# Chunk outputs formed transposed on TensorE, in place of transposes after them, in a delta-rule attention and FFN kernel

## The chip, the cores and the metric

One Trainium2 chip, one core. The metric is the device time of one execution in microseconds (us). Engines are named as in the profile: PE is TensorE, PEld its weight loads, DVE VectorE, ACT ScalarE, POOL GpSimd, SP the engine whose queue issues all DMAs here.

## The reference

Attention with a delta-rule state, then a feed-forward layer, in float32. Sizes: batch B = 4, heads H = 8, sequence S = 768, head size D = 48; 3072 tokens, model width 384, hidden width 2048.

```python
for t in range(S):
    kt, vt, bt = (k_n[:, :, t], v[:, :, t], beta[:, :, t, None])
    y[:, :, t] = np.einsum('bhd,bhde->bhe', q[:, :, t], state)
    v_old = np.einsum('bhde,bhd->bhe', state, kt)
    state = state + bt[:, :, :, None] * np.einsum('bhd,bhe->bhde', kt, vt - v_old)
...
h = x @ w_in
sp = np.maximum(h, 0.0) + np.log1p(np.exp(-np.abs(h)))
g = h * erf(sp)
return (g @ w_out).astype(np.float32)
```

`x` is `y` with the heads of a token side by side (384 features).

## The kernel before

**Tiling.** The sequence is cut into 12 chunks `c` of C = 64 steps. Within a chunk the recurrence is solved as a triangular system, so that a chunk of one batch entry, `j = 4c + b`, 48 in all, needs three sets of small fp32 products: `chain_u` (line 490), `chain_s` (503, the new state) and `chain_y` (517, the output). The 8 heads of a `j` are 4 pairs `p` times 2 halves `hb`; the two halves stand on partitions 0 to 63 and 64 to 127. Four `j` (one chunk of all four batch entries, 256 tokens) make one FFN group `g`, 12 in all.

**FFN.** Each f32 operand is scaled by a power of two and split in two f16 parts. `ffn1` (16 steps of each group) is 9 f16 matmuls of 128x256 (line 707: high by high, high by low, low by high, for 3 k-tiles); `ffn2` (16 steps) is 6 of 128x384 (lines 768 to 770). Between them, for a unit of two steps: `e_sp` (softplus, ACT), `h_out` (copy out of PSUM, DVE or ACT), `e_erf` (ACT), `e_mul` (DVE), `e_split` (f16 high part), `e_rest` (f16 low part, mostly POOL). Softplus and erf lie in different ACT tables; `table()` (line 129) loads one where the last step used the other, so the number of loads follows from the order of steps.

**From chunk output to FFN input, which the change touches.** `chain_y` has `qp` as its 64-column stationary operand and the state and values `zz` as moving operand, so tokens come out on partitions: 8 fp32 matmuls of 128x48 (16 in the trace, as an fp32 matmul is two there), into two column halves of 64. `chain_y2` (522, ACT) copies the 128x192 result out, `chain_m` (528, DVE) takes its largest magnitude per partition. For a group, `x_max`, `x_all` (552, a product that spreads the maxima) and `x_scale` give the scale `sx`. FFN needs features on partitions: `x_tr` (673, 674) transposes with 8 fp32 PE transposes per group, into 2 PSUM banks from the pool `psa` of 3; `x_hi` (690, ACT) and `x_lo` (695, DVE) form the f16 parts from PSUM, each in 6 pieces per group (2 of 128x256, 4 of 64x128).

**Order.** Every step is put in a list (`on(time, function, arguments)`), 2511 steps; the tuple `ORDER` then gives the order in which they are issued. Each engine and the SP queue works through its own instructions strictly in that order; semaphores alone hold it back. 150 `fill` steps are idle matmuls in the first 90 us. Time of a step in `on(...)` has no effect once `ORDER` is there.

Of the kernel before, what the change touches and what calls it, by code (L numbers as in the profile page):

```python
# [7 lines left out]
F32 = mybir.dt.float32  # L8
# [48 lines left out]
YR = 6  # L57
# [12 lines left out]
HSC = 2.0 ** -23  # L70


@with_exitstack
def delta_ffn_kernel(ctx, tc, kT, qT, ktok, vtok, btok, w_in, w_out, cst, out):
    nc = tc.nc
    te, ve, se, ge, sp = nc.tensor, nc.vector, nc.scalar, nc.gpsimd, nc.sync

    con = ctx.enter_context(tc.tile_pool(name="con", bufs=1))
    io = ctx.enter_context(tc.tile_pool(name="io", bufs=2))
    at = ctx.enter_context(tc.tile_pool(name="at", bufs=1))  # L80
    sm = ctx.enter_context(tc.tile_pool(name="sm", bufs=3))
    ff = ctx.enter_context(tc.tile_pool(name="ff", bufs=2))
# [23 lines left out]
    zz = [con.tile([P, NP, 2, D], F32, name=f"z{i}") for i in range(6)]  # L106

    wb = {nm: con.tile([P, NFF + 1, DM], F32, name=f"w_{nm}") for nm in ("in", "out")}
    wv = {nm: w.rearrange("p a b -> p (a b)").bitcast(F16).rearrange("p (a k b) -> p a k b", k=2, b=DM) for nm, w in wb.items()}
    (win_h, win_l), (wout_h, wout_l) = ((v[:, :, 0, :], v[:, :, 1, :]) for v in wv.values())  # L110

    def early(off, n):

        return wb["out"].rearrange("p a b -> p (a b)")[:, off:off + n]

    def r(hb):
        return slice(hb * C, hb * C + C)

# [329 lines left out]
    def merge_m(c, i):  # L448
# [15 lines left out]
    ygrp, mg = {}, {}  # L464
    vt = {}

    def load_v(j):
        c, b = divmod(j, B)
        vt[j] = io.tile([P, NP, D], F32, tag="v", bufs=2, name=f"v{j}")
        sp.dma_start(vt[j], vtok[c][:, b * NP:b * NP + NP, :])  # L470

    def put_v(j):
        c, b = divmod(j, B)
        cs = slice(b * NP, b * NP + NP)
        for hb in range(2):
            h1 = r(1 - hb)
            ge.tensor_tensor(zz[j % 6][h1, :, hb, :], vt[j][h1], st[c]["nm"][h1, cs].unsqueeze(2).broadcast_to([C, NP, D]), op=ALU.mult)  # L477
# [3 lines left out]
    def chain_u(j):  # L481
        c, b = divmod(j, B)
        Z = zz[j % 6]
        pc = pr[j % PB] if j < 2 * B else pbank(f"pc{j}")
        pu = pc[:, :192].rearrange("p (a e) -> p a e", a=NP)
        psn = pc[:, 192:384].rearrange("p (a e) -> p a e", a=NP)
        pcs[j] = pc, pu, psn
        for p in range(NP):
            for hb in range(2):
                te.matmul(pu[r(1 - hb), p, :], xm[c % 2][hb][:, b * NP + p, :], Z[:, p, hb, :], start=True, stop=True)  # L490

    def chain_u2(j):
# [176 lines left out]
    def x_tr(g, i):  # L669
        y = ygrp[g]  # L670
        pv = fg[g]["pt", i] = pbank(f"pt{g}_{i}").rearrange("p (a x) -> p a x", a=2)
        for a in range(2):
            te.transpose(pv[:, a, :P], y[2 * i + a][:, :P], ident)
            te.transpose(pv[:C, a, P:], y[2 * i + a][:, P:], ident)

    def x_parts(g, i):
        G = fg[g]
        pv = G["pt", i]
        js = slice(2 * i, 2 * i + 2)
        return (((slice(0, P), js, slice(0, P)), pv[:, :, :P]),  # L680
                ((slice(0, C), js, slice(P, 192)), pv[:C, :, P:P + C]),
                ((slice(C, P), js, slice(P, 192)), pv[:C, :, P + C:]))

    def x_hi(g, i):
# [7 lines left out]
    def x_lo(g, i):
        G = fg[g]
        for dst, src in x_parts(g, i):
            ve.scalar_tensor_tensor(G["xl"][dst], src, G["sx"][:src.shape[0]], G["xh"][dst], op0=ALU.mult, op1=ALU.subtract)  # L695

    def ffn1(n):
        g, i = divmod(n, NFF)
        G = fg[g]
        if ("ph", i // 2) not in G:  # L700
            G["ph", i // 2] = ps1.tile([P, 2, GT], F32, tag="ph", name=f"ph{g}_{i // 2}")
        ph = G["ph", i // 2][:, i % 2, :]
        m = 0
        for kt in range(3):
            ksl = slice(kt * C, kt * C + C)
            for w, x in ((win_h, "xh"), (win_h, "xl"), (win_l, "xh")):
                te.matmul(ph, w[:, i, kt * P:kt * P + P], G[x][:, :, ksl], start=(m == 0), stop=(m == 8))  # L707
                m += 1
# [190 lines left out]
    for j in range(B * NC_):  # L899
        t = chain_at(j)  # L900
        d = 1.0 if j >= 2 * B else 2.6 / SW / CS
        on(t - 3.3 if j >= 2 * B else t - 1.5, load_v, j)
        on(t - 1.2 if j >= 2 * B else t - 0.7, put_v, j)
        on(t, chain_u, j)
        on(t + 0.2 * d, chain_u2, j)
        if j < B * NC_ - B:
            on(t + CS * d, chain_s, j)
            on(t + (CS + 0.25) * d, chain_s2, j)
        on(t + (CS + 0.05) * d, chain_y, j)
        on(t + (CS + 0.3) * d, chain_y2, j)  # L910
        on(t + (CS + 0.7) * d, chain_m, j)
# [117 lines left out]
```

## Time and profile before

| | us |
|---|---|
| median of 3 runs (669.54 to 673.52) | 670.56 |
| the profiled execution | 671.37 |
| its span, first to last instruction | 669.6 |
| PE busy, of the span | 605.9 |
| DVE busy | 487.1 |
| ACT busy | 447.7 |
| POOL busy | 364.1 |

The first `ffn1` is at 103.7 us, the first `ffn2` at 138.2, the last matmul at 664. A busy PE is counted to the modelled end of each matmul, some 0.2 us after its start, so that short stops between matmuls lie inside the busy time; the spacing of starts shows them.

### The profile page before, as it was taken

What the parts mean: (1) busy time and instruction counts of PE and PEld (TensorE: products, weight loads), DVE (VectorE), ACT (ScalarE), POOL (GpSimd) and SP (SyncE); (2) the same over time, 40 slices, a digit from 0 to 9 for tenths busy, and PEclk for the clock granted to TensorE, in tenths of its full rate; (3) what the DMA queues carried; (4) which work ended last, traced back from release to release, by engine and by line L of the source; (5) the groups of instructions that cost most, each with busy time, mean ns of one, the idle gap of its engine ahead of it and who ended that gap; (6) DMA issues with size and microseconds to landing.
All of it is one profiled execution on the core that took longest, in us unless ns stands there. A gap on an engine that the chain in (4) does not pass through costs nothing.

```text
span 669.6 us, 22927 instructions
## 1 busy us (share of the span) xinstructions
PE 605.9 (90%) x9866; PEld 457.9 (68%) x9866; DVE 487.1 (73%) x1032; ACT 447.7 (67%) x678; POOL 364.1 (54%) x524
## 2 busy tenths in 40 slices
PE   6947898888988989989999999899999999999996
PEld 4634665667775667767777777677677787777674
DVE  4987689897887877888987587676577876554442
ACT  2345697877766735749647878777738858578673
POOL 4172049858689646994359872678663420140222
PEclk9877899999998999989999999999999999999999
DMA  9982592349220287131793122623404410000111
GB/s 240 328 228 78 140 235 52 80 100 173 66 56 2 54 182 153 48 82 34 179 147 75 44 45 49 136 43 85 102 2 94 96 37 14 13 14 1 24 37 24
DMA packets 78981, 60.13 MB, mean 90 GB/s; under 512 B 57504, under 2 KB 66848, under 8 KB 78880
## 3 DMA queue, kind: packets, MB, share of 16 engines
q1 hardware_dynamic: 78880, 58.68, 37.2%
q8 instruction: 77, 1.26, 0.8%
q14 instruction: 24, 0.20, 0.1%
HBM read 46.07 MB, written 12.58 MB: 88 GB/s over the span
## 4 chain that ended last, share of the span: by engine, by line
PE 48%; DVE 25%; ACT 11%; issue 7%; POOL 4%; DMA 3%; SPq 1%; DVEq 0%; ACTq 0%; POOLq 0%
PE ph L707 16%; PE pr L768 5%; PE pr L770 5%; PE pr L769 5%; DVE H L742 4%; DVE H L720 3%; ACT L L733 2%; PE pc L517 2%; PE pc L490 2%; DVE L L753 2%; ACT L129 2%; PE pc L503 2%; POOL xb L393 2%; POOL tmp L392 1%; PE pz L442 1%
## 5 line engine op out<-in xcount | busy, mean ns | idle before, releaser
L707 PE MATMUL ph<-xh,w_in 128*128 128x256 f16 x1152 | 209.5, 274 | 14.3 <-DVE H L720 6.4
L707 PEld LDWEIGHTS <-w_in 128*128 128x128 f16 x1728 | 167.2, 98 | 45.3 <-issue 18.6
L757 POOL TENSOR_TENSOR L<-H,L 128x512 f16<-128x512 f32 x72 | 88.0, 1233 | 163.6 <-DVE L L753 107.1
L707 PE MATMUL ph<-xl,w_in 128*128 128x256 f16 x576 | 157.7, 274 | 0.0
L129 ACT ACT_TABLE_LOAD x115 | 147.5, 1283 | 2.0
L769 PE MATMUL pr<-w_out,L 128*128 128x384 f16 x384 | 125.5, 327 | 2.8 <-DVE w_out L644 2.8
L768 PE MATMUL pr<-w_out,L 128*128 128x384 f16 x384 | 125.6, 327 | 1.6 <-ACT ob L778 1.6
L770 PE MATMUL pr<-w_out,L 128*128 128x384 f16 x384 | 125.6, 327 | 0.0
L733 ACT ACTIVATE L<-ph,xct 128x512 f32<-128x512 f32 x96 | 65.3, 687 | 67.3 <-DVE H L720 41.6
L393 POOL TENSOR_TENSOR xb<-xb,tmp 128x31 f32<-128x31 f32 (+15 forms) x155 | 95.3, 615 | 12.2
L392 POOL TENSOR_TENSOR tmp<-gb,xb 128x31 f32<-128x31 f32 (+15 forms) x155 | 87.6, 565 | 25.3 <-DMA gb<-d 15.2
L477 POOL TENSOR_TENSOR z<-v,nm 64x192 f32<-64x192 f32 x96 | 57.2, 596 | 78.2 <-DMA v<-vtok 67.6
L742 DVE TENSOR_TENSOR H<-H,L 128x512 f32<-128x512 f32 x96 | 73.6, 771 | 21.1 <-ACT L L738 20.5
L720 DVE TENSOR_SCALAR H<-ph 128x512 f32<-128x512 f32 x72 | 49.1, 685 | 46.5 <-ACT L L733 19.7
L738 ACT ACTIVATE L<-L 128x512 f32<-128x512 f32 x96 | 58.9, 627 | 0.8
L770 PEld LDWEIGHTS <-L 128*128 128x128 f16 x384 | 37.6, 98 | 27.8 <-issue 3.2
L769 PEld LDWEIGHTS <-L 128*128 128x128 f16 x384 | 37.6, 98 | 21.7 <-issue 2.0
L768 PEld LDWEIGHTS <-L 128*128 128x128 f16 x384 | 37.6, 98 | 21.2 <-issue 0.2
L753 DVE CAST L<-H 128x512 f16<-128x512 f32 x72 | 43.3, 611 | 0.8
L511 DVE TENSOR_TENSOR z<-pc,z 48x192 f32<-48x192 f32 x72 | 25.5, 354 | 16.6 <-PE pc L517 7.9
L496 DVE TENSOR_TENSOR z<-pc,ga 64x192 f32<-64x192 f32 x80 | 28.3, 354 | 11.3 <-PE pc L490 7.7
L695 DVE SCALAR_TENSOR_TENSOR xl<-pt,xsx,xh 64x128 f16<-64x128 f32 (+1 forms) x72 | 25.8, 385 | 13.4 <-ACT xh L690 12.8
(159 smaller groups left out, 973.8 us busy)
## 6 DMA issues: line engine op xcount, KB each, us to landing
raw_in<-w_in SPq DMA_DIRECT2D x12, 512.0 KB, 8.5
raw_out<-w_out SPq DMA_DIRECT2D x12, 512.0 KB, 6.3
d<-A SPq DMA_DIRECT2D x20, 256.0 KB, 3.5
k<-ktok SPq DMA_DIRECT2D x12, 384.0 KB, 5.0
kpg<-kT SPq DMA_DIRECT2D x24, 192.0 KB, 5.0
qp<-qT SPq DMA_DIRECT2D x24, 192.0 KB, 4.9
v<-vtok SPq DMA_DIRECT2D x48, 96.0 KB, 3.2
out<-ob SPq DMA_DIRECT2D x48, 96.0 KB, 2.2
```

The source lines that it names most:

```text
L129: se.add_instruction(mybir.InstLoadActFuncSet(name=nc.get_next_instruction_name(), act_func_set_id=i, ins=[], outs=[]))
L392: ge.tensor_tensor(tv, G[:, s, s + 1:].unsqueeze(1).broadcast_to([P, ncol, nr]), Xv[:, :, s:s + 1].broadcast_to([P, ncol, nr]), op=ALU.mult)
L393: ge.tensor_tensor(Xv[:, :, s + 1:], Xv[:, :, s + 1:], tv, op=ALU.add)
L707: te.matmul(ph, w[:, i, kt * P:kt * P + P], G[x][:, :, ksl], start=(m == 0), stop=(m == 8))
L720: ve.tensor_scalar(dst, src, HSC, None, op0=ALU.mult)
L733: se.activation(unit("L", g, u), G["ph", u], AF.Softplus, bias=0.0, scale=G["ct"])
L738: se.activation(Lu, Lu, AF.Erf, bias=0.0, scale=1.0)
L742: ve.tensor_tensor(Hu, Hu, unit("L", g, u), op=ALU.mult)
L757: (ge if (g * NFF // EU + u) % GLM else ve).tensor_tensor(G["gl", u], unit("H", g, u), G["gh", u], op=ALU.subtract)
L768: te.matmul(G["po"][a], gh[:, o, asl], wout_h[:, i, :], start=(i == 0), stop=False)
L769: te.matmul(G["po"][a], gh[:, o, asl], wout_l[:, i, :], start=False, stop=False)
L770: te.matmul(G["po"][a], gl[:, o, asl], wout_h[:, i, :], start=False, stop=(i == NFF - 1))
```

## The change

1. `chain_y` swaps its operands: 32 columns of `zz` are the stationary operand and `qp` (64 steps) is moving, so features come out on partitions. It is 16 fp32 matmuls of 128x64 (32 in the trace) in place of 8, into four column quarters of 32 partitions in turn. The list `YS` says which features go where; the last 8 matmuls add two and two into one place. For this `zz` has its heads 64 apart, with 16 columns of zeros.
2. `x_tr` is gone. `chain_y2` copies 128x192 as before, but into `xt`, one SBUF tile of 128x768 per group (2 buffers).
3. `chain_m` runs once for two `j`, over 384 values.
4. `x_hi` and `x_lo` are one instruction each per group, over 128x768, from SBUF.
5. `ffn1` reads 256 adjacent columns, not 4 times 64. The rows of `w_in` are laid out anew on the host.
6. `ORDER` is another permutation, now of 2439 steps. Nothing else changes in what a step does.

Counted in the two lists of steps:

| | before | after |
|---|---|---|
| changes of the PE tile shape from one PE step to the next (128x128, 128x64, 128x32, 64x64, 32x32), whole kernel | 206 | 250 |
| the same before the first `ffn1` | 42 | 45 |
| `chain_u` right next to `chain_y` | 19 | 6 |
| ACT table loads | 115 | 103 |
| of these for groups 0 to 4 and 5 to 11 | 37, 76 | 44, 58 |
| `ffn` steps between the last `x_all` or `x_tr` of a group and its first `ffn1`, groups 1 to 11 | 3 to 23, mean 9.8 | 2 to 12, mean 6.6 |
| DMA issues on SP | 209 | 209 |

On SP the first issues are, before: k of chunks 0 and 1, beta, both `kpg`; after: k of chunk 0 and 1, `kpg` of chunk 0, k of chunk 2 (384 KB), `kpg` of chunk 1, q of chunk 0, beta.

```diff
+YS = [(m % 4, m // 4, m // 2, m % 2, m // 2 * C + 16 * (m // 2 % 2), True, True) for m in range(8)]
+YS += [(s, 2, s // 2 * 2 + x, s % 2, s // 2 * 2 * C + 32 + 16 * x, not x, bool(x)) for x in range(2) for s in range(4)]
...
-    zz = [con.tile([P, NP, 2, D], F32, name=f"z{i}") for i in range(6)]
+    zz = [con.tile([P, 2, NP, C], F32, name=f"z{i}") for i in range(6)]
...
     def chain_y(j):
         c, b = divmod(j, B)
-        for p in range(NP):
-            for hb in range(2):
-                te.matmul(pcs[j][1][r(1 - hb), p, :], qp[c % 2][hb][:, b * NP + p, :], zz[j % 6][:, p, hb, :], start=True, stop=True)
+        py = pcs[j][0][:, :3 * C].rearrange("p (k t) -> p k t", k=3)
+        zf = zz[j % 6].rearrange("p h a d -> p h (a d)")
+        for n, (s, kt, p, hb, x, first, last) in enumerate(YS):
+            te.matmul(py[32 * s:32 * s + 32, kt, :], zf[:, hb, x:x + 32], qp[c % 2][hb][:, b * NP + p, :], start=first, stop=last)
 
     def chain_y2(j):
         g, js = divmod(j, GS)
-        y = ygrp.setdefault(g, {})[js] = at.tile([P, NP * D], F32, tag="y", bufs=YR, name=f"y{j}")
-        se.copy(y, pcs[j][0][:, :192])
+        if g not in xt:
+            xt[g] = at.tile([P, 3, GT], F32, tag="xt", bufs=YR, name=f"xt{g}")
+        se.copy(xt[g][:, :, js * C:js * C + C], pcs[j][0][:, :3 * C].rearrange("p (k t) -> p k t", k=3))
 
     def chain_m(j):
...
-        ve.tensor_reduce(mg[g][:, js:js + 1], ygrp[g][js], axis=AX.X, op=ALU.max, apply_absolute_value=True)
+        ve.tensor_reduce(mg[g][:, js // 2:js // 2 + 1], xt[g][:, :, (js - 1) * C:(js + 1) * C], axis=AX.XY, op=ALU.max, apply_absolute_value=True)
...
-    def x_tr(g, i):
-        y = ygrp[g]
-        pv = fg[g]["pt", i] = pbank(f"pt{g}_{i}").rearrange("p (a x) -> p a x", a=2)
-        for a in range(2):
-            te.transpose(pv[:, a, :P], y[2 * i + a][:, :P], ident)
-            te.transpose(pv[:C, a, P:], y[2 * i + a][:, P:], ident)
...
-        for dst, src in x_parts(g, i):
-            se.activation(G["xh"][dst], src, AF.Copy, bias=0.0, scale=G["sx"][:src.shape[0]])
...
+        se.activation(G["xh"], xt[g], AF.Copy, bias=0.0, scale=G["sx"])
...
+        ve.scalar_tensor_tensor(G["xl"], xt[g], G["sx"], G["xh"], op0=ALU.mult, op1=ALU.subtract)
...
-                te.matmul(ph, w[:, i, kt * P:kt * P + P], G[x][:, :, ksl], start=(m == 0), stop=(m == 8))
+                te.matmul(ph, w[:, i, kt * P:kt * P + P], G[x][:, kt, :], start=(m == 0), stop=(m == 8))
```

## Rows read from the trace of the kernel before

**Rows 1.** The page, part 1: busy us, share of the span, instructions.

```profile
PE 605.9 (90%) x9866; PEld 457.9 (68%) x9866; DVE 487.1 (73%) x1032; ACT 447.7 (67%) x678; POOL 364.1 (54%) x524
```

**Rows 2.** Busy time by stretch: length, then us (x instructions) of PE, PEld, DVE, ACT, POOL.

```profile
0.00:139.00 139.00, 107.68 (x2235) 76.19 (x2236) 109.58 (x259) 84.49 (x154) 71.62 (x110) 0.90 0.61 169
139.00:325.00 186.00, 168.50 (x2975) 130.84 (x2972) 151.60 (x302) 126.97 (x195) 134.89 (x191) 0.98 0.41 88
325.00:601.00 276.00, 266.79 (x4214) 207.40 (x4215) 198.16 (x418) 192.67 (x276) 144.80 (x213) 1.00 0.32 68
601.00:669.60 68.60, 62.96 (x446) 43.44 (x444) 27.72 (x54) 43.60 (x55) 12.77 (x10) 0.98 0.09 21
```

**Rows 3.** Waits of PE, 139 to 664.5 us: total us, times, longest.

```profile
PE ph L707 <- DVE H L720: 5.2, 6, 1.9
PE ph L707 <- ACT L L733: 3.9, 6, 1.4
PE pr L769 <- DVE w_out L644: 2.8, 1, 2.8
PE pq L276 <- DVE qp L303: 1.9, 1, 1.9
...
PE pr L768 <- ACT ob L778: 1.6, 1, 1.6
PE pc L503 <- issue: 1.4, 1, 1.4
```

**Rows 4.** Timeline of PE at 456 us: start, us, engine, line, operation.

```profile
456.00 0.27 PE L707 MATMUL ph<-xh,w_in 128*128 128x256 f16 x1
456.11 0.27 PE L673 MATMUL pt<-ident,y 128*128 128x128 f32 x1
...
456.54 0.33 PE L768 MATMUL pr<-w_out,L 128*128 128x384 f16 x1
```

**Rows 5.** Timeline of PE at 303 us.

```profile
302.48 0.33 PE L769 MATMUL pr<-w_out,L 128*128 128x384 f16 x1
302.64 0.33 PE L770 MATMUL pr<-w_out,L 128*128 128x384 f16 x1
302.90 0.67 PE L517 MATMUL pc<-z,qp 128*64 128x48 f32 x16
303.40 0.64 PE L490 MATMUL pc<-z,xm 128*64 128x48 f32 x16
303.97 0.34 PE L768 MATMUL pr<-w_out,L 128*128 128x384 f16 x1
```

**Rows 6.** Timeline of PE from 9.9 us: the first Gram products, 32-column stationary operands.

```profile
10.11 1.98 PE L248 MATMUL pg<-kpg 48*32 48x64 f32 x124 [0.61 <-DMA kpg<-kT]
16.52 0.26 PE L248 MATMUL pg<-kpg 48*32 48x64 f32 x1 [4.44 <-issue]
```

**Rows 7.** Groups by line and shape, DVE and ACT: count, busy us, mean ns, idle before.

```profile
L695 DVE SCALAR_TENSOR_TENSOR xl<-pt,xsx,xh 64x128 f16<-64x128 f32 x48 | 16.2, 338 | 0.4
L528 DVE TENSOR_REDUCE mg<-y 128x1 f32<-128x192 f32 x48 | 15.6, 345 | 6.9 <-ACT y L522 6.7
L644 DVE SCALAR_TENSOR_TENSOR w_out<-w_out,sc_out 128x384 f16<-128x384 f32 x16 | 14.3, 891 | 2.0 <-ACT w_out L619 1.8
...
L695 DVE SCALAR_TENSOR_TENSOR xl<-pt,xsx,xh 128x256 f16<-128x256 f32 x24 | 11.5, 479 | 13.0 <-ACT xh L690 12.8
...
L129 ACT ACT_TABLE_LOAD x115 | 147.5, 1283 | 2.0
...
L690 ACT ACTIVATE xh<-pt,xsx 64x128 f16<-64x128 f32 x48 | 17.1, 357 | 0.3
...
L690 ACT ACTIVATE xh<-pt,xsx 128x256 f16<-128x256 f32 x24 | 11.3, 471 | 11.0 <-PE pt L674 6.7 <-DVE xsx L557 3.4 <-DVE xct L663 0.8
...
L184 ACT ACTIVATE sq<-k 128x768 f32<-128x768 f32 x10 | 8.4, 843 | 10.9 <-DVE n L192 6.2 <-DMA k<-ktok 4.7
```

**Rows 8.** The chain that ended last, its first long piece: start, us, what.

```profile
3.54 6.53 DMA kpg<-kT
```

More of the change, by code (lines that the diff above doesn't have):

```diff
@@ L56 @@
 XR = 3
-YR = 6
+YR = 2
 S2A = (0, 1, 2, 3)
@@ L462, in merge_m2 @@
             ve.tensor_scalar(dst, src, -1.0, None, op0=ALU.mult)
-    ygrp, mg = {}, {}
+    xt, mg = {}, {}
     vt = {}
@@ L476, in put_v @@
             h1 = r(1 - hb)
-            ge.tensor_tensor(zz[j % 6][h1, :, hb, :], vt[j][h1], st[c]["nm"][h1, cs].unsqueeze(2).broadcast_to([C, NP, D]), op=ALU.mult)
+            ge.tensor_tensor(zz[j % 6][h1, hb, :, :D], vt[j][h1], st[c]["nm"][h1, cs].unsqueeze(2).broadcast_to([C, NP, D]), op=ALU.mult)
     pcs = {}
@@ L489, in chain_u @@
             for hb in range(2):
-                te.matmul(pu[r(1 - hb), p, :], xm[c % 2][hb][:, b * NP + p, :], Z[:, p, hb, :], start=True, stop=True)
+                te.matmul(pu[r(1 - hb), p, :], xm[c % 2][hb][:, b * NP + p, :], Z[:, hb, p, :D], start=True, stop=True)
     def chain_u2(j):
@@ L495, in chain_u2 @@
             h1 = r(1 - hb)
-            ve.tensor_tensor(zz[j % 6][h1, :, hb, :], pcs[j][1][h1],
+            ve.tensor_tensor(zz[j % 6][h1, hb, :, :D], pcs[j][1][h1],
                              st[c]["ga"][h1, b * NP:b * NP + NP].unsqueeze(2).broadcast_to([C, NP, D]), op=ALU.mult)
@@ L502, in chain_s @@
             for hb in range(2):
-                te.matmul(pcs[j][2][rd(hb), p, :], st[c]["k"][r(1 - hb), b * NP + p, :], zz[j % 6][r(1 - hb), p, hb, :], start=True, stop=True)
+                te.matmul(pcs[j][2][rd(hb), p, :], st[c]["k"][r(1 - hb), b * NP + p, :], zz[j % 6][r(1 - hb), hb, p, :D], start=True, stop=True)
     def chain_s2(j):
         for hb in range(2):
-            dst, new = zz[(j + B) % 6][rd(hb), :, hb, :], pcs[j][2][rd(hb)]
+            dst, new = zz[(j + B) % 6][rd(hb), hb, :, :D], pcs[j][2][rd(hb)]
             if j in S2A:
@@ L510, in chain_s2 @@
             else:
-                ve.tensor_tensor(dst, new, zz[j % 6][rd(hb), :, hb, :], op=ALU.add)
+                ve.tensor_tensor(dst, new, zz[j % 6][rd(hb), hb, :, :D], op=ALU.add)
     def chain_y(j):
         c, b = divmod(j, B)
-        for p in range(NP):
-            for hb in range(2):
-                te.matmul(pcs[j][1][r(1 - hb), p, :], qp[c % 2][hb][:, b * NP + p, :], zz[j % 6][:, p, hb, :], start=True, stop=True)
+        py = pcs[j][0][:, :3 * C].rearrange("p (k t) -> p k t", k=3)
+        zf = zz[j % 6].rearrange("p h a d -> p h (a d)")
+        for n, (s, kt, p, hb, x, first, last) in enumerate(YS):
+            te.matmul(py[32 * s:32 * s + 32, kt, :], zf[:, hb, x:x + 32], qp[c % 2][hb][:, b * NP + p, :], start=first, stop=last)
     def chain_y2(j):
         g, js = divmod(j, GS)
-        y = ygrp.setdefault(g, {})[js] = at.tile([P, NP * D], F32, tag="y", bufs=YR, name=f"y{j}")
-        se.copy(y, pcs[j][0][:, :192])
+        if g not in xt:
+            xt[g] = at.tile([P, 3, GT], F32, tag="xt", bufs=YR, name=f"xt{g}")
+        se.copy(xt[g][:, :, js * C:js * C + C], pcs[j][0][:, :3 * C].rearrange("p (k t) -> p k t", k=3))
     def chain_m(j):
@@ L526, in chain_m @@
         if g not in mg:
-            mg[g] = sm.tile([P, GS], F32, tag="mg", name=f"mg{g}")
-        ve.tensor_reduce(mg[g][:, js:js + 1], ygrp[g][js], axis=AX.X, op=ALU.max, apply_absolute_value=True)
+            mg[g] = sm.tile([P, 2], F32, tag="mg", name=f"mg{g}")
+        ve.tensor_reduce(mg[g][:, js // 2:js // 2 + 1], xt[g][:, :, (js - 1) * C:(js + 1) * C], axis=AX.XY, op=ALU.max, apply_absolute_value=True)
     NRW = 3 * DFF // RW
@@ L667, in x_scale2, with x_hi, x_lo @@
         ve.tensor_tensor(G["co"], G["m2"], c_out, op=ALU.mult)
-    def x_tr(g, i):
-        y = ygrp[g]
-        pv = fg[g]["pt", i] = pbank(f"pt{g}_{i}").rearrange("p (a x) -> p a x", a=2)
-        for a in range(2):
-            te.transpose(pv[:, a, :P], y[2 * i + a][:, :P], ident)
-            te.transpose(pv[:C, a, P:], y[2 * i + a][:, P:], ident)
-    def x_parts(g, i):
-        G = fg[g]
[L678 to L684, printed above, removed]
-        G = fg[g]
-        if "xh" not in G:
-            G["xh"] = ff.tile([P, GS, 192], F16, tag="xh", bufs=XR, name=f"xh{g}")
-            G["xl"] = ff.tile([P, GS, 192], F16, tag="xl", bufs=XR, name=f"xl{g}")
-        for dst, src in x_parts(g, i):
-            se.activation(G["xh"][dst], src, AF.Copy, bias=0.0, scale=G["sx"][:src.shape[0]])
[L692 to L695, printed above, removed]
+    def x_hi(g):
+        G = fg[g]
+        G["xh"] = ff.tile([P, 3, GT], F16, tag="xh", bufs=XR, name=f"xh{g}")
+        G["xl"] = ff.tile([P, 3, GT], F16, tag="xl", bufs=XR, name=f"xl{g}")
+        se.activation(G["xh"], xt[g], AF.Copy, bias=0.0, scale=G["sx"])
+    def x_lo(g):
+        G = fg[g]
+        ve.scalar_tensor_tensor(G["xl"], xt[g], G["sx"], G["xh"], op0=ALU.mult, op1=ALU.subtract)
     def ffn1(n):
@@ L704, in ffn1 @@
         for kt in range(3):
-            ksl = slice(kt * C, kt * C + C)
             for w, x in ((win_h, "xh"), (win_h, "xl"), (win_l, "xh")):
-                te.matmul(ph, w[:, i, kt * P:kt * P + P], G[x][:, :, ksl], start=(m == 0), stop=(m == 8))
+                te.matmul(ph, w[:, i, kt * P:kt * P + P], G[x][:, kt, :], start=(m == 0), stop=(m == 8))
                 m += 1
@@ L910, in delta_ffn_kernel @@
         on(t + (CS + 0.3) * d, chain_y2, j)
-        on(t + (CS + 0.7) * d, chain_m, j)
+        if j % 2:
+            on(t + (CS + 0.7) * d, chain_m, j)
     for i in range(NRW):
@@ L957, in delta_ffn_kernel @@
         on(max(x0 + 0.3 * d, WO + WD * NRW + 1.6), x_scale2, g)
-        for i in range(GS // 2):
-            on(x0 + (0.2 + 0.5 * i) * d, x_tr, g, i)
-            on(x0 + (0.5 + 0.5 * i) * d, x_hi, g, i)
-            on(x0 + (0.7 + 0.5 * i) * d, x_lo, g, i)
+        on(x0 + 0.5 * d, x_hi, g)
+        on(x0 + 0.7 * d, x_lo, g)
         for i in range(NFF):
@@ L1007, in layout @@
     hd = NP * D
-    rows = np.concatenate([np.arange(hd, hd + P), np.arange(0, P), np.arange(hd + P, 2 * hd), np.arange(P, hd)])
+    rows = np.empty((3, 4, 32), np.int64)
+    for s, kt, p, hb, x, _, _ in YS:
+        for m in range(32):
+            f = x + m - p * C
+            if 0 <= f < D:
+                rows[kt, s, m] = hb * hd + p * D + f
+    rows = rows.reshape(-1)
     w_in = np.ascontiguousarray(moe_w_in[rows].reshape(3, P, NFF, P).transpose(1, 2, 0, 3)).reshape(P, -1).view(np.int64)
```

2 lines of the change are left out of this document (1 added, 1 removed).

## Prediction

> **What bounds the kernel now.** I read the page's busy times first, then the busy time by stretch, then the waits of PE in the FFN stretch, then the timeline around single steps. The page shows PE busy for 90% of the span, DVE for 73%, ACT for 67% [rows 1]: PE leads, and the two that feed it are not far. By stretch [rows 2] it is three kernels. To 139 us (loads, first solve, preparation of the weights) PE stands 31.3 us, and its busy time holds the idle `fill` matmuls: there the chain through DMA, DVE and ACT decides. From 139 to 325 us PE stands 186 - 168.5 = 17.5 us and DVE is busy 151.6 of 186 (82%). From 325 to 601 us PE stands 9.2 of 276 us, at a granted clock of 1.00 (2.4 GHz): PE is the bound. In the last 68.6 us it stands 5.6, most of it after its last matmul. The waits say for whom it stood from 139 us on [rows 3]: copies and splits on DVE (5.2 + 2.8 + 1.9 us in the largest three), softplus and output on ACT (3.9 + 1.6). So in the FFN part a microsecond of PE work is worth nearly a microsecond, and work taken off DVE or ACT is worth only the waits that it shortens.
>
> **The transposes.** Four of them start at 456.11 us and the next `ffn2` at 456.54 [rows 4]: 0.43 us for a burst, with no gap on either side, as they have the same 128x128 shape as FFN. There are 24 bursts, all in a PE that is mostly full: 24 x 0.43 = 10.3 us off.
>
> **The new `chain_y`.** Before, the 16 matmuls of one `j` take 303.40 - 302.90 = 0.50 us until the next step starts, 31 ns each [rows 5]; the two column halves overlap. After, there are 32 matmuls with 64 moving columns. The nearest row is the first Gram product, which also has 32-column stationary operands and 64 moving columns, placed in all four column quarters: 124 of them last 1.98 us, less some 0.2 for the modelled end of the last 1.76 us, 14.3 ns each [rows 6]. It differs in one thing, since its operands have 48 rows and lie in two row halves, and here all 128 rows feed all four quarters. At 14.3 ns a `j` costs 32 x 0.0143 = 0.46 us, 48 of them -1.9 us against now; at 31 ns, where no more than two quarters overlap, 0.99 us, +24 us. I take 0.50, no change: the row with the same stationary and moving widths is near it, and the other would need the overlap to stop at two.
>
> **Changes of shape.** This is what the profile charges against the change. From `ffn2` to `chain_y` the start comes 302.90 - 302.64 = 0.26 us later, against 0.16 within `ffn2`: +0.10. From `chain_y` to `chain_u`, of the same shape, 0.50 us; from `chain_u`, as many matmuls, to `ffn2` 303.97 - 303.40 = 0.57: +0.07 [rows 5]. With 32 columns `chain_y` no longer has the shape of `chain_u`, and the new order changes shape 250 times, not 206. 44 x 0.07 to 0.10 is 3.1 to 4.4 us; I take 4. PE together: -10.3 + 0 + 4 = -6.3 us.
>
> **DVE and ACT.** `x_lo` goes from 16.2 + 11.5 = 27.7 us to 12 instructions of 768 elements. The growth from 128 to 256 elements is (479 - 338)/128 = 1.1 ns per element, so 0.479 + 512 x 0.0011 = 1.04 us each; the same kind from SBUF, on `w_out`, took 0.891 us for 384, so 1.78 at the most [rows 7]. I take 1.2: 14.4 us, 13.3 less (6.3 to 15.2). `chain_m`: 48 x 0.345 = 16.6 to 24 x (0.345 + 192 x 0.0011) = 13.4, 3.2 less. `x_hi`: 17.1 + 11.3 = 28.4 to 12 x 0.843 (the square of 768 elements) = 10.1, 18.3 less. 12 table loads of 1.283: 15.4 less, though groups 0 to 4 get 7 more (+9.0) [rows 7]. DVE then has 16.5 us less and ACT 33.7. What is it worth? The waits of PE on them named above are 15.4 us [rows 3]. I take 6 off, between nothing (in a fixed order a faster step only moves the stop) and all: the DVE-bound stretch is early, where DVE loses about 5 of 151.6 us and ACT gains table loads, and ACT's large relief is late, where PE hardly waits. `chain_y2` stays 192 elements, and costs nothing new. The larger clearing of `zz` on POOL lies in the start, beside DMA waits. `ffn1` with adjacent columns I cost at nothing, below nothing by little: its spacing of 0.11 us [rows 4] leaves a strided read no visible price.
>
> **What is late next.** `x_tr` did not need the scale, so half the old way was done before it. Now `x_all`, `x_scale`, `x_hi` and `x_lo` stand one behind another: the 0.84 and 1.2 us from above, behind the small instructions of `x_all` and `x_scale`, which were there before too: over 2 us without queueing. Behind `x_hi` on ACT wait `e_sp` and `e_erf`, behind `x_lo` on DVE `h_out` and `e_mul`, and PE waits for those as [rows 3] shows. The cover is the `ffn` steps until the group's first `ffn1`, 2 to 12 of them, on average 6.6, at 9 x 0.11 = 1.0 us [rows 4]: enough on average, thin in places.
>
> **The start.** Two groups' DVE savings (2 x 1.4 = 2.8 us) lie in a stretch that waits for DVE. Against them, SP now has the 384 KB of chunk 2 ahead of `kpg` of chunk 1, and the first Gram products wait for `kpg` [rows 8]: 384 KB behind the 1536 KB that came first is a quarter more, 6.53/4 = 1.6 us. The new order of SP and POOL further on I can't price by rows; both move loads far ahead of their use. I take -1 (-5 to +5).
>
> **The sum** against the profiled execution: 671.4 - 6.3 (PE) - 6 (waits) - 1 (start) = 658.1 us. The median of the runs is 0.8 below that execution, so 657 us, 2% less. Its own range is 649 to 663.
>
> **Rivals.**
> *Bigger gain:* the order takes most of the waits away, 15.4 rather than 6, and the DVE savings of the start count in full with a few us of its 31 us of standing: 657 - 9 - 4 = 644. For it, 33.7 us off ACT and idle PE at the start; against it, more table loads in the early groups. 0.15.
> *PE alone:* the waits stay, since what DVE and ACT gain goes into the stops at group starts where the cover is thin; half a us for each of 11 groups is enough. 671.4 - 6.3 - 0.8 = 664, or 667 where the start loses its 1 and more: no measurable change, taking 1% of 670.6, 6.7 us, as what a measurement tells from none. 0.25.
> *The small products don't come closer than now (slower):* the place is `chain_y`. If four quarters fed by the same 128 rows do not overlap beyond two, a `j` costs 32 x 0.031 = 0.99 us; the price is +24 us, 681 us. It decides from +0.28 us per `j` (13.4/48) on, 24 ns per matmul. Against it, 14.3 ns in [rows 6]; for it, no row has four quarters on the same rows. 0.09. The Trainium skill (TensorE: Matmul & The Clock Gate, "Wait — 56ns, not 53.3ns?") says that matmuls never start less than about 25 ns apart, however small. By that alone a `j` would take an estimated 0.80 us, the sum +14 us, 671 us; the 14.3 ns of [rows 6] contradict it for overlapping quarters, so it has its part in the 0.09 and no more. The page on TensorEngine Tiling (Array Packing), "Theoretical Speedup", gives up to four times for 32 columns; no row of this kernel shows that with all 128 rows.
> *Instruction supply:* in [rows 6] PE stops for 4.44 us after 124 quick matmuls, waiting for nothing that the profile shows; from 139 us on there is one such stop that counts, 1.4 us [rows 3]. `chain_y` issues 768 matmuls and as many weight loads more, at twice the rate. One more stop of 1.4 us for each of 12 chunks is +17: 674 us, no measurable change. 0.06.
>
> **How the numbers follow.** 0.45 for the forecast, 0.15, 0.25, 0.09 and 0.06 for the rivals. Faster by over 1% (under 663.9 us): 0.45 + 0.15 and a little of the second rival, 0.62. Within 1%: 0.28. Slower: 0.10. The range of 8 in 10 leaves out the slow rival and a little of the biggest gain: 642 to 675 us.
>
> **What would show it.** Right: no group at `x_tr`; `chain_y` x1536 with starts near 14 to 16 ns and bursts of 0.5 us; `x_hi` at 0.85 and `x_lo` near 1.2 us; 103 table loads; DVE near 470 and ACT near 414 us busy; PE's standing from 139 us on down by some 6 us. Wrong: `chain_y` bursts of 0.8 us and more; new "issue" stops on PE; waits of `ffn1` for `x_lo`, or longer waits for `h_out` and softplus; a first `ffn1` stream that starts later than now.

## The result and the profile after

The changed kernel takes 631.3 us (median of 4 runs, 626.1 to 635.5) against 672.0 for the kernel before beside it: ratio 0.938, 95% interval 0.928 to 0.947. Timed once more later, it took 630.9 us (627.7 to 636.6), ratio 0.940 (0.936 to 0.944). That is 6% faster; the forecast was 657 us, 2%, and 631 lies below its range (649 to 663) and below the wider one of 8 in 10 (642 to 675). The profiled execution (626.1 us, span 624.3) is the fastest of the first four. For runs 5, 7 and 8 below, the ratio is that of the means against eleven of the thirteen runs of the kernel before beside them (673.3 us), since the other two were slow.

The page of the changed kernel, part 1, answers to [rows 1]:

```profile
PE 594.8 (95%) x10538; PEld 445.6 (71%) x10538; DVE 465.5 (75%) x948; ACT 417.1 (67%) x606; POOL 371.2 (59%) x524
```

Its busy time by stretch, with the columns of [rows 2]:

```profile
0.00:139.00 139.00, 121.46 (x2587) 85.62 (x2588) 115.50 (x261) 94.02 (x160) 86.07 (x127) 0.90 0.71 193
139.00:325.00 186.00, 180.14 (x3497) 139.16 (x3495) 155.38 (x301) 137.77 (x193) 143.50 (x205) 1.00 0.42 95
325.00:601.00 276.00, 275.03 (x4342) 209.52 (x4343) 190.08 (x382) 179.74 (x246) 137.73 (x191) 1.00 0.24 54
601.00:624.30 23.30, 18.14 (x118) 11.28 (x116) 4.53 (x6) 5.55 (x7) 3.86 (x4) 0.97 0.15 35
```

Length of a stretch less PE's busy time is what PE stood. Before it was 31.3, 17.5, 9.2 and 5.6 us [rows 2]; now it is 17.5, 5.9, 1.0 and 5.2. So the span's 45.3 us (669.6 - 624.3) are 11.1 of PE's work (605.9 - 594.8) and 34 of PE's standing: 13.8 in the start and 19.8 from 139 to 601 us. The stretches are equal in time, not in work; counted from the first `ffn2` to the last matmul, PE stands 8.2 us now and stood 27.2. Not all of the 11.1 us need be fewer matmuls: from 139 to 325 us the granted clock is 1.00 against 0.98 before, and run 1 below, with the same 10538 matmuls in the old order, keeps PE busy for 598.5 us. To 139 us every engine now does more in the same time: DVE 115.5 against 109.6 us, ACT 94.0 against 84.5, POOL 86.1 against 71.6.

The largest waits of PE from 139 us on, against [rows 3]:

```profile
PE pc L494 <- issue: 1.6, 1, 1.6
PE pc L507 <- DVE z L500: 1.4, 1, 1.4
PE pc L494 <- ACT xm L464: 1.0, 2, 0.8
```

The waits of `ffn1` for `h_out` and softplus, 9.1 us in [rows 3], are not in the list any more. The sizes that the prediction worked out, in the groups by line (busy us, mean ns | idle before):

```profile
L133 ACT ACT_TABLE_LOAD x103 | 132.1, 1283 | 1.8
L534 DVE TENSOR_REDUCE mg<-xt 128x1 f32<-128x384 f32 x24 | 13.0, 544 | 2.9 <-ACT xt L528 2.8
L683 DVE SCALAR_TENSOR_TENSOR xl<-xt,xsx,xh 128x768 f16<-128x768 f32 x12 | 12.7, 1056 | 5.3 <-ACT xh L679 5.3
L679 ACT ACTIVATE xh<-xt,xsx 128x768 f16<-128x768 f32 x12 | 11.2, 933 | 9.8 <-DVE xsx L563 5.3 <-DVE xct L669 4.4
```

And the new `chain_y` in PE's timeline, three `j` behind one another, which answers to [rows 5]:

```profile
272.13 0.33 PE L757 MATMUL pr<-w_out,L 128*128 128x384 f16 x1
272.38 1.55 PE L522 MATMUL pc<-qp,z 128*32 128x64 f32 x96
273.86 0.92 PE L507 MATMUL pc<-z,k 64*48 64x48 f32 x32
```

A `j` takes (273.86 - 272.38)/3 = 0.49 us, 15 ns for each of the 32 records; from `ffn2` to it 0.25 us, of which 0.16 is the spacing within `ffn2`. These are the prediction's 0.50 and 0.26.

### The profile page after: what moved, and what is told of

It reads as the page before. It is cut to its first block, busy times and chain, and to the rows that moved or that the text cites. A ratio compares the mean times of both kernels' runs of the same rounds, so it can differ in the third digit from the quotient of the medians.

```text
span 624.3 us, 24082 instructions
## 1 busy us (share of the span) xinstructions
PE 594.8 (95%) x10538; PEld 445.6 (71%) x10538; DVE 465.5 (75%) x948; ACT 417.1 (67%) x606; POOL 371.2 (59%) x524
## 4 chain that ended last, share of the span: by engine, by line
PE 65%; DVE 14%; ACT 12%; issue 3%; DMA 3%; POOL 1%; SPq 1%; DVEq 0%; ACTq 0%; POOLq 0%
PE ph L694 23%; PE pr L755 8%; PE pr L757 8%; PE pr L756 8%; PE pc L494 3%; ACT L133 3%; PE pc L522 3%; PE pz L446 2%; DMA kpg<-kT 2%; PE pc L507 2%; PE pe L433 2%; PE pq L280 2%; DVE L L740 2%; ACT L L725 1%; PE pm L278 1%
## 5 line engine op out<-in xcount | busy, mean ns | idle before, releaser
L694 PE MATMUL ph<-xh,w_in 128*128 128x256 f16 x1152 | 206.9, 273 | 1.0 <-ACT w_in L646 1.0
L396 POOL TENSOR_TENSOR tmp<-gb,xb 128x31 f32<-128x31 f32 (+15 forms) x155 | 88.4, 571 | 19.8 <-DMA gb<-d 10.0
L729 DVE TENSOR_TENSOR H<-H,L 128x512 f32<-128x512 f32 x96 | 77.4, 817 | 23.7 <-ACT L L725 22.8
L481 POOL TENSOR_TENSOR z<-v,nm 64x192 f32<-64x192 f32 x96 | 62.6, 652 | 42.0 <-DMA v<-vtok 24.3
L725 ACT ACTIVATE L<-L 128x512 f32<-128x512 f32 x96 | 57.3, 625 | 0.6
L740 DVE CAST L<-H 128x512 f16<-128x512 f32 x72 | 40.7, 571 | 1.1
L500 DVE TENSOR_TENSOR z<-pc,ga 64x192 f32<-64x192 f32 x80 | 28.4, 355 | 14.4 <-PE pc L494 12.7
L148 PE MATMUL warm<-zero 128*128 128x384 f16 x158 | 34.6, 371 | 1.1 <-DVE zero L139 1.1
L464 ACT ACTIVATE xm<-pm 48x512 f32<-48x512 f32 x28 | 16.4, 591 | 22.4 <-PE pq L280 18.3
```

The source lines that it names most:

```text
L396: ge.tensor_tensor(tv, G[:, s, s + 1:].unsqueeze(1).broadcast_to([P, ncol, nr]), Xv[:, :, s:s + 1].broadcast_to([P, ncol, nr]), op=ALU.mult)
L481: ge.tensor_tensor(zz[j % 6][h1, hb, :, :D], vt[j][h1], st[c]["nm"][h1, cs].unsqueeze(2).broadcast_to([C, NP, D]), op=ALU.mult)
L694: te.matmul(ph, w[:, i, kt * P:kt * P + P], G[x][:, kt, :], start=(m == 0), stop=(m == 8))
L725: se.activation(Lu, Lu, AF.Erf, bias=0.0, scale=1.0)
L729: ve.tensor_tensor(Hu, Hu, unit("L", g, u), op=ALU.mult)
```

## The experiments

The median of the kernel before lay between 672.0 and 675.7 us beside the different runs, so variants are compared by their ratio to the runs of before made beside them; a thousandth of the ratio is 0.67 us. The changed kernel has 0.940.

**1 and 2. The code without the order, and the order without the code.** Run 1 has the new code and the old `ORDER`, with `x_hi` and `x_lo` at the places of their first pieces and `chain_m` at that of the later `j`; run 2 has the old code in the new `ORDER`, with the pieces at the place of `x_hi` or, where three banks of `psa` do not allow that, close to it.

```diff
-ORDER = (new permutation)
+ORDER = (old permutation without x_tr, new steps at the places told)
...
-ORDER = (old permutation)
+ORDER = (new permutation with x_tr and the pieces)
-YR = 6
+YR = 8
```

> The changed kernel with the order of before: each step stands where it stood, x_tr steps fall out, x_hi and x_lo of a group stand at the place of their first piece, chain_m at the place of the later of its two. Theory 'order': the 45 us of the profiled runs are mostly the new order, and the new code in the old order is worth what the forecast summed, 655 to 662 us, with PE waits from 139 us on near the 27 us of before. Theory 'code': fewer instructions on DVE and ACT and no transposes empty the waits in any order, 630 to 642 us, with PE idle near 30 us in all.

> The kernel of before with the new order: both chain_m of a pair stand where the one stands, x_tr, x_hi and x_lo of a half group stand together near the place of x_hi, the second half two FFN steps later where a PSUM bank is free (8 y buffers, not 6). Theory 'order': about 10 us of transposes, 16 of DVE work and 18 of ACT work come back into an order without slack for them, 640 to 650 us. Theory 'code': 662 us or more.

New code in the old order: 666.3 us, 0.989 (0.985 to 0.993). Old code in the new order: 676.8 us, 1.004 (1.000 to 1.007). Neither half holds the gain: the one gives 1% (a little less than theory 'order' expected), the other nothing, both together 6%. Busy time of the first by stretch, in the two FFN stretches:

```profile
139.00:325.00 186.00, 171.33 (x3369) 132.23 (x3367) 152.93 (x290) 127.29 (x185) 137.93 (x191) 0.99 0.44 97
325.00:601.00 276.00, 263.27 (x4437) 201.23 (x4435) 186.89 (x375) 187.68 (x248) 145.91 (x213) 0.99 0.29 62
```

PE stands 14.7 and 12.7 us, 27.4 together, against 26.7 in [rows 2]. It has 7.4 us less to do (598.5 of busy time against 605.9), and this alone comes out at the end. The relief of DVE and ACT is there (471.0 and 432.9 us busy) and moves nothing. The waits of PE in the second, from 139 us on:

```profile
PE pt L673 <- DVE xl L695: 4.2, 3, 2.4
PE pc L490 <- DVE xl L695: 4.2, 2, 2.4
PE pm L274 <- DVE xl L695: 3.4, 2, 2.0
...
PE pq L276 <- DVE xl L695: 3.0, 2, 2.2
...
PE ph L707 <- DVE xl L695: 1.5, 2, 0.9
```

Four of the five are no readers of `xl`: transposes, chain products and Gram products wait until `x_lo` gives back a PSUM bank. The old `x_tr` held two of the three banks of `psa` from the transposes to `x_lo`, and the new order has its other users come close behind.

**3. `chain_y` without neighbours in different quarters.** The list is sorted, so that the matmuls of one column quarter stand together.

```diff
+YS = sorted(YS, key=lambda m: m[0])
```

> The changed kernel with the 16 matmuls of chain_y sorted by column quarter, four in a row into the same quarter, so that neighbours can't overlap. If the 14.0 ns spacing comes from overlap of the four quarters, a matmul then takes 64 columns in two passes, 56 ns, a j 32 x 0.056 = 1.8 us instead of 0.45, and PE, the bound, gets 48 x 1.34 = +64 us: about 690 us. If the spacing is set by issue alone, nothing changes.

One run: 652.9 us. A burst in the timeline:

```profile
302.44 1.39 PE L523 MATMUL pc<-qp,z 128*32 128x64 f32 x32
303.77 1.16 PE L270 MATMUL pg<-kpg 48*64 48x64 f32 x64
```

A `j` now takes 1.33 us to the next step (about 1.2 by its own starts) against 0.49. So it is the interleaving of quarters that makes the small products cheap, by some 0.7 us x 48 = 34 us of PE time (its busy time is 625.4 us, 31 more), of which some 20 came out at the end. The expectation was too large because the sorted matmuls start 37 ns apart and not 56; why, no run shows.

**4, 5, 11, 12, 16. The old work put back into the new order, part by part.** Run 4 puts eight transposes per group back on PE, into unused columns of the bank of `x_all`. Run 11 makes `x_hi` in six pieces from SBUF, run 12 `x_lo` in six and `chain_m` per `j`, run 5 all three, run 16 all three and the transposes. What the transposes write is read by nobody.

```diff
+        for i in range(8):
+            te.transpose(bank[:, P * (1 + i % 3):P * (2 + i % 3)], xt[g][:, i % 3, P * (i // 4):P * (i // 4) + P], ident)
...
-        se.activation(G["xh"], xt[g], AF.Copy, bias=0.0, scale=G["sx"])
+        for i in range(2):
+            for ps, ks in ((slice(0, P), slice(0, 2)), (slice(0, C), slice(2, 3)), (slice(C, P), slice(2, 3))):
+                w = slice(i * P, i * P + P)
+                se.activation(G["xh"][ps, ks, w], xt[g][ps, ks, w], AF.Copy, bias=0.0, scale=G["sx"][ps])
```

> The changed kernel with the 8 transposes of a group put back as PE work alone, behind x_all, into unused columns of its bank; nobody reads them. If PE bounds the changed kernel, their 96 x 0.109 = 10.5 us come back whole: 1.6% longer, 641 us against 631. If there were slack on PE, it would be under 0.8%.

> The changed kernel in its own order, with x_hi, x_lo and chain_m back in the piece sizes of before (6, 6 and, per pair of chunks, 2 instructions), all from SBUF: the old ACT and DVE work (some 17 and 16 us more) without the old PE work and without PSUM. Theory 'relief': the order is free of stops only because DVE and ACT have less to do, so 10 us or more come back, 641 us and over. Theory 'PSUM': what hurt the old code in the new order is that PE waited for x_lo to free the banks of the transposes; then this costs under 5 us, 632 to 636 us.

> The changed kernel with x_hi alone in six pieces per group (2 of 128x256 and 4 of 64x128, from SBUF), so that ACT has some 17 us more and DVE nothing. With all three steps in pieces the time was 651.7 against 631.3 us. Theory 'ACT': it is ACT that PE waits for in the new order, 645 to 650 us. Theory 'DVE': 630 to 635. Theory 'queue': each of the two lengthens the same chain from scale to first ffn1 and each alone costs about half, 638 to 643.

> The changed kernel with x_lo in six pieces per group and chain_m once per j, x_hi as one instruction, so that DVE has some 19 us more and ACT nothing. Theory 'DVE': it is DVE that PE waits for in the new order, 645 to 650 us. Theory 'ACT': 630 to 635. Theory 'queue': each alone about half of the 20 us, 638 to 643.

> The changed kernel with x_hi and x_lo in six pieces and chain_m once per j (651.7 us), and the eight transposes per group back on PE into a bank that nothing else waits for. The whole old code in the new order took 676.8 us. Theory 'sum with banks': the transposes add their 4 to 10 us, 656 to 662, and the other 15 to 20 us of the old code are the two PSUM banks that it held from x_tr to x_lo (PE waited 16.5 us for x_lo in it). Theory 'late chain': what costs is PE's transposes and the pieces behind one another, the banks add nothing: 670 to 677.

| in the new order | median us | ratio (interval) | above 0.940, x 672 us |
|---|---|---|---|
| 4: transposes on PE | 635.7 | 0.944 (0.941 to 0.948) | +3 |
| 11: `x_hi` in pieces, ACT | 642.2 | 0.955 (0.951 to 0.958) | +10 |
| 12: `x_lo`, `chain_m` in pieces, DVE | 646.3 | 0.958 (0.954 to 0.963) | +12 |
| 5: both | 651.7 | 0.966 (0.961 to 0.972) | +18 |
| 16: both, and transposes | 650.8 | 0.969 (0.966 to 0.973) | +20 |
| 2: the whole old code | 676.8 | 1.004 (1.000 to 1.007) | +43 |

The relief on DVE and ACT, worth nothing in the old order, is worth 18 us in the new one, and each half alone costs 10 to 12, as the theory 'queue' has it (run 12's 646 us lies above its range): the two steps lie in one chain, and a delay anywhere in it holds up the first `ffn1`. From the start of `x_scale` to the end of `x_lo` a group takes 7.5 us on average in run 5, against 5.0 in the changed kernel. With run 12 PE's waits from 139 us on show that place:

```profile
PE ph L698 <- DVE xl L687: 3.9, 4, 1.7
PE ph L698 <- DVE H L711: 3.9, 3, 2.8
```

The transposes cost 3 us alone and 2 on top of the pieces, under the 10.3 of PE time that they take; part of it fills time in which PE stood (from 139 to 601 us 3.7 us in run 4, some 7 in the changed kernel). They are not PE's work alone: `x_scale` reads the same bank, and in most groups it starts 1.3 us behind `x_all` in place of 0.4, when the transposes are through. Run 16 lies below both of its expected ranges. From run 16 to run 2 there are 23 us more with nearly the same work. What differs is that the old code reads `x_hi` and `x_lo` out of the two banks, and that the transposes stand behind one another with them. The 16.3 us of PE's waits for `x_lo` above speak for the banks; no run takes them alone, and the two profiles, run 2's fastest and run 16's slowest execution (670.0 and 659.8 us), are only 10 us apart.

**6 and 7. Softplus and the copy from the same bank.** In the trace, ACT's softplus and DVE's `h_out` of a unit never run at once; the later one waits. ACT's waits for `h_out` in the kernel before:

```profile
ACT L L733 <- DVE H L720: 41.6, 20, 6.2
```

The same in run 1, the new code in the old order:

```profile
ACT L L720 <- DVE H L707: 42.5, 19, 6.2
```

And in the changed kernel:

```profile
ACT L L720 <- DVE H L707: 14.3, 6, 6.6
```

This falls with the stops of PE, so it could be their cause. Run 6 takes run 1 and issues `h_out` behind the softplus of its unit wherever it stood ahead; run 7 takes the changed kernel and issues it ahead, in 39 units of groups 3 to 11.

> The changed kernel in the order of before, but in the 44 of 96 units where h_out stood ahead of e_sp it now stands right behind it; nothing else moves. The two read the same PSUM bank and run one after the other in the order of issue. Theory 'pair': ACT stood 42 us behind DVE's copies in the old order (14 in the new), and this is what made the stops of PE; then most of ACT's wait goes and 10 us or more with it, 656 us and under against 666. Rival 'many small things': the wait turns into one of DVE on ACT, and the time stays within 4 us of 666.

> The changed kernel in its own order, but in 39 units of groups 3 to 11 h_out, which stood behind e_sp, now stands right ahead of it. Theory 'pair': ACT's wait on the copies grows from 14 us to 40 and more and 10 us or more come back, over 641 us. Rival: under 4 us, 632 to 636 us.

Run 6: 674.0 us, 1.001 (0.998 to 1.004), slower than run 1 and outside both of its ranges. Run 7: 636.9 us, 0.945 (0.941 to 0.950), some 4 us above the changed kernel at most, although its waits of ACT, in the same view, are longer than before:

```profile
ACT L L720 <- DVE H L707: 52.5, 24, 6.6
```

So the theory fell. The Trainium skill (PSUM — Partial Sum Buffer, "PSUM bank collisions raise a hardware error") says that accesses of two engines to one bank on the same partitions have to be kept apart; the trace agrees, but 38 us more of this wait cost some 4 us at most.

**8, 9, 10. The start.** Run 8 has the steps ahead of the first `ffn2` in the old order and all behind it in the new. Run 9 is the changed kernel with the four steps of 128 tiny products each (`first_w`, `first_x`) put behind one another as before, and run 10 is run 8 with these four set apart by `fill` steps as in the new order.

```diff
-first_w:0, fill, first_x:0, fill x5, first_w:1, first_x:1
+fill x6, first_w:0, first_w:1, first_x:0, first_x:1
```

> The changed kernel with the steps that the new order has ahead of its first ffn2 (635 of 2439) put into the sequence they have in the old order, and the new order from there on. If the 14 us by which the first ffn2 comes earlier (123.6 against 138.2 us) are the order's and are carried to the end by a PE that is full from there on, 640 to 646 us. If the start only loses what the rest would have waited anyway, 631 to 635 us.

> The changed kernel, with one thing of the start's order put back: the two trains of 128 tiny products each of first_w and of first_x stand one behind another (first_w of both chunks, then first_x of both), as in the order before, and the six idle fill matmuls that lay between them go ahead of them. The code, the loads and all later steps are as changed. Theory 'supply': PE cannot run through such trains faster than its instructions come; the fills and the waits for ACT between the trains cover that. Then stops with no releaser of 4 to 6 us come back between 36 and 60 us (they were 4.2, 6.0 and 2.5 us before, 0.6 and 1.2 after), the first ffn2 is 5 to 8 us later than 124 us, and the time is 636 to 641 us against 631. Theory 'loads': the start's gain comes from the order of the loads and of DVE's work, and PE has slack here: the first ffn2 stays within 2 us, the time at 629 to 634.

> The kernel with the old start order and the new order behind the first ffn2 (652.2 us), and in it the one thing of the new start: one fill between first_w of chunk 0 and first_x of chunk 0, five fills between that and first_w of chunk 1, first_x of chunk 1 last; the fills are taken from just ahead. Theory 'supply': the stops of 3.6, 6.3 and 2.5 us with no releaser shrink to 1 to 2 us each, the first ffn2 comes 5 to 8 us earlier than 136 us, and the time is 644 to 648. Theory 'loads': the stops may shrink, but the first ffn2 stays within 2 us and the time at 650 to 654.

Run 8: 652.2 us, 0.969 (0.966 to 0.972), +20 us, more than either range had. Run 9: 634.3 us, 0.943 (0.939 to 0.946), +2. Run 10: 652.0 us, 0.969 (0.966 to 0.973), the same as run 8. The stops with no releaser do come back in run 9, 128 matmuls apart in PE's timeline:

```profile
42.66 0.41 PE L373 MATMUL pw<-w_out 16*32 16x16 f32 x16 [3.40 <-issue]
42.90 1.13 PE L384 MATMUL pw<-w_out 32*16 32x16 f32 x111
48.13 1.27 PE L384 MATMUL pw<-w_out 32*16 32x16 f32 x128 [4.11 <-issue]
51.58 0.31 PE L384 MATMUL pw<-w_out 32*16 32x16 f32 x17 [2.18 <-issue]
```

In the profiles the first `ffn2` is then at 132 us instead of 124; the time is hardly longer. In run 10 the stops in these trains are 7.8 us instead of the 12.3 of run 8, and its first `ffn2` stays at 136 us. So 'supply' explains stops and not the time. What run 8 does show is one long wait of PE, at 144 us:

```profile
PE pe L433 <- DVE T L424: 13.0, 3, 12.3
```

`merge_e` of chunk 2 waits for the solve of chunks 2 and 3, 31 rows on POOL that take 42 us. Its first row is at 97.5 us here, at 95.0 before, and at 78.8 in the changed kernel.

**14 and 17. Only the solve earlier.** Both are run 8 with the feeding steps of this solve (`norm_ops`, `gram_two`, `gram_a`, `to_dram`, `to_blocks`, `solve_row`, the load of `kpg`) at their new places; run 17 has `load_v` and `put_v` there too. In run 17 `put_v` of `j` = 7 fills a `zz` that the products of `j` = 1 have still to read, so these take other values; their number and size stay, but POOL does not wait for them, as it would have to for the right values.

> The kernel with the old start order and the new order behind the first ffn2 (652.2 us), and in it only the steps that feed the solve of chunks 2 and 3 on POOL moved to the places that they have in the new start: the last three of norm_ops, gram_two, gram_a, to_dram and to_blocks of these chunks, solve_row, the load of their kpg, and first_x2 of chunk 1 as far as its PSUM bank needs it. Theory 'solve': the new start is worth what it brings the solve forward; the first row of the solve moves from 97.5 us towards 80 to 85, PE's wait of 12 us for it at 144 us is gone or below 2 us, and the time is 636 to 644 us. Theory 'weights': the start ends when the weights are ready, and the stalled PE would only have waited for them; the wait goes, and the time stays at 648 to 653.

> The kernel with the old start order and the new order behind the first ffn2 (652.2 us), with the steps that feed the solve of chunks 2 and 3 at their new places as in e14 (652.8 us), and now also every load_v and put_v of the start at its new place, so that POOL, which works in order, does not stand before the solve waiting for v. Theory 'solve': the first row of the solve moves from 97.5 us to 80 to 88, PE's wait of 10 to 12 us for the merge of chunk 2 falls below 3 us, and the time is 638 to 645 us; what is then left to 631 us is the first ffn2, some 8 us later. Theory 'weights': the first ffn1 and ffn2 stay where they are (106 and 137 us), the wait goes, and the time stays at 648 to 653 us, since PE only waits elsewhere.

Run 14: 652.8 us, 0.973 (0.969 to 0.976), nothing gained. POOL's timeline shows why:

```profile
92.28 3.02 POOL L481 TENSOR_TENSOR z<-v,nm 64x192 f32<-64x192 f32 x4 [14.24 <-DMA v<-vtok]
95.27 0.23 POOL L396 TENSOR_TENSOR tmp<-gb,xb 128x31 f32<-128x31 f32 x1
```

The table of the solve was issued 9 us earlier than in run 8 (79.5 against 88.9), but POOL stood 14.24 us at a `put_v`, ahead of the solve in its queue, for a `v` that the old start loads late. Run 17 frees it: the first row is at 90.7 us, the wait of 10 us for chunk 2 is gone, and the time is 646.2 us, 0.955 (0.950 to 0.960), some 9 us less than run 8 by the ratios (6 by the medians; its times fall into two groups, 641 to 643 and 649 to 650 us, and the profile is of the second). But its first `ffn2` is at 144 us, 7 later than in run 8: what comes forward for the solve pushes the weights back. About 10 us of the start's gain stay open.

**13 and 15. Again, and the new start with the old rest.**

> The changed kernel, nothing altered, beside the next three on one chip. Its four runs spread from 626.1 to 635.5 us and the profile is of the fastest, with the first ffn2 at 124 us; kernels with the same start order had it between 125 and 131. If the spread lies in the start, this profile's first ffn2 stands between 124 and 132 us and the median at 630 to 634 us.

> New code throughout, the new order up to the first ffn2 and the old order behind it. With new code, old start and old rest took 666.3 us, old start and new rest 652.2, new start and new rest 631.3. Theory 'sum': the two parts of the order add up, and the new start is worth about 20 us here too: 645 to 650 us. Theory 'fit': the old rest issues its steps at the old distances, and waits until the late ones come; the start alone is worth under 8 us: 658 to 666.

Run 13 is the 0.940 used above; its first `ffn2` is at 128 us. Of the ten profiles beside the first that keep the new start whole (runs 2 to 5, 7, 11 to 13, 15, 16), nine have it between 125 and 133 us and run 16, in its slowest execution, at 137: the 124 of the first profile is the best case, and some 10 us is nearer to what the start usually gains by then. Run 15: 661.4 us, 0.984 (0.980 to 0.988). Its FFN stretches:

```profile
139.00:325.00 186.00, 168.38 (x3327) 129.76 (x3325) 149.47 (x284) 122.57 (x178) 133.68 (x189) 0.97 0.41 91
325.00:601.00 276.00, 263.27 (x4446) 201.34 (x4442) 186.97 (x375) 188.56 (x250) 145.91 (x213) 1.00 0.30 63
```

PE stands 17.6 and 12.7 us there. With the new code, old start and old rest make 0.989, the new start alone 0.984, the new rest alone 0.969, both 0.940: 0.6 and 2.0 points singly, 4.9 together. 'Fit' holds: the parts of the order do not add up, each is worth most with the other.

## Why the prediction was wrong

**Right.** The sizes. `chain_y` 0.49 us per `j` for 0.50; transposes 24 x 0.43 us of PE time (run 4 has 606.5 us of PE busy time against 594.8 and 597.3 in the two profiles of the changed kernel); `x_lo` 1.06 us for 1.2, `chain_m` 0.544 for 0.556, `x_hi` 0.93 for 0.84; 103 table loads; DVE 465.5 and ACT 417.1 us busy for 470 and 414. The PE sum of -6.3 us is what run 1 shows by itself: PE busy 7.4 us less, 0.989, 7 us; in the changed kernel PE has 11.1 us less, 8.6 in its second profile. The rival "PE alone" (664 to 667) is the time of the new code in the old order, 666.3. Its term of 4 us for changes of shape no run takes by itself, and one reading behind it is not right: two of the four transposes of a burst [rows 4] have a tile of another shape than FFN's, in the same timeline of the kernel before:

```profile
456.22 0.27 PE L674 MATMUL pt<-ident,y 128*64 128x128 f32 x1
```

They start 0.11 us behind their neighbours like the rest, so a change of shape does not cost 0.07 to 0.10 us everywhere.

**The waits, "I take 6 off": this step failed.** It had two faults. Its upper bound was the 15.4 us of the named waits in [rows 3], though [rows 2] gave 26.7 us of standing from 139 to 601 us; 19.8 of it went (18.7 in the second profile). And it valued a step's relief as if the order were fixed, though the change brings another. In the old order that value was right, even too high: nothing (run 1). In the new order the same relief is worth 18 us (run 5).

**The banks: a term left out.** That `x_tr` leaves two of three PSUM banks of `psa` free stands in the kernel, and the sum has nothing for it. In the new order the old code with its banks costs 23 us more than nearly the same work without them (runs 16 and 2); 16.3 us of PE's waits in run 2 are for these banks, the rest is not told apart.

**The start, "I take -1": failed.** PE stood 13.8 us less there (12.0 in the second profile), and with the new rest the start is worth 20 us (run 8). The step priced single moves on the SP queue (+1.6 us) and found no rows for the others. What it passed over is that the second solve on POOL starts 16 us earlier (78.8 against 95.0 us). Bringing it forward by 7 us, together with the loads of `v`, gave some 9 us (run 17); the rest of the start's gain is not traced to a step.

**The late chain** of `x_all` to `x_lo`: right. PE waits for `x_lo` 0.4 us in all. It becomes the tight place as soon as a step in it grows (run 12).

**The rivals.** "Bigger gain" (0.15) had the direction and a reason that holds, but its 15.4 and 4 us were bounded by the same too small numbers. The slow rival, quarters fed by the same rows, did not occur; its price per `j` (0.99 us) was about right for a list that does not interleave them (about 1.2, run 3). "Instruction supply" did not occur: from 139 us on, stops with no releaser are 2.3 us, 2.6 before. The Trainium skill (TensorE: Matmul & The Clock Gate, "Wait — 56ns, not 53.3ns?") has no two starts closer than about 25 ns; the 15 ns above contradict it for four quarters in turn.

**Open.** Which placements of the new order keep PE from standing in the FFN part was not found; the pairing of softplus and copy is not it (runs 6, 7). Whether the old code could gain as much from an order of its own was not tried; the new order does nothing for it.

## What to carry to other kernels

Where each engine works in a fixed order, a shorter step can be worth little until the order is made anew around it (here 1% of 6), and an order that fits one code may do nothing for another: price code and order together, and take as the upper bound all that the bounding engine stands, not only the waits that are named. Look at what a removed step held (here PSUM banks) as well as at what it did. When a chain is brought forward, look at every queue it passes: in run 14 a wait for a load of `v` in POOL's queue left no gain at all.

## What was not expected of the hardware

Stops of PE with no releaser come at fixed places in its instruction stream. In PE's timeline of the kernel before, in the start, 128 tiny matmuls lie between two of them:

```profile
51.93 1.27 PE L380 MATMUL pw<-w_out 32*16 32x16 f32 x128 [5.99 <-issue]
55.66 0.34 PE L380 MATMUL pw<-w_out 32*16 32x16 f32 x19 [2.45 <-issue]
```

In run 9 they come back at the same distance (4.11 and 2.18 us above); where `fill` matmuls and waits for ACT stand between the trains, as in the changed kernel, they are 1.2 us at most in these trains in its first profile and 2.8 in its second.

The traces show what ends them. The pages have a DMA queue for instructions, with its packets, MB and share, first in the kernel before, then in the changed one:

```profile
q8 instruction: 77, 1.26, 0.8%
q8 instruction: 83, 1.36, 0.9%
```

That is a packet of 16 KB for every 256 and 254 of PE's records, a matmul and its weight load counted as two. In the trace of the kernel before such packets end at 14.9, 43.1, 50.7, 54.3 and 77.0 us, and the stops of over 2 us end at 16.5, 44.5, 51.9, 55.7 and 78.5 us. Of 93 such stops of over 0.9 us in all the traces, 89 end 1.2 to 1.7 us behind the end of such a packet. So PE stands there for its next portion of instructions, and semaphores are not all that holds it back. What makes a portion late, no run tried.
